# A delta rule and a feed-forward block on one core: the first pair's feed-forward in plain fp32, its weights split a pair later

## The chip, the core and the metric

The kernel runs on one core of a Trainium2 chip. The core has five engines that run side by side: TensorE (PE in the profile; its weight loads are PEld), VectorE (DVE), ScalarE (ACT), GpSimd (POOL) and SyncE (SP), which here only issues DMAs. Each engine goes through its own list of instructions in order and waits on semaphores. The metric is the device time of one execution in microseconds, the median of several; lower is better.

## The reference

Two steps. First a delta rule: for each of 32 sequences (4 batches of 8 heads) a 48 x 48 state is read and updated 768 times.

```python
for t in range(S):
    y[:, :, t] = np.einsum('bhd,bhde->bhe', q[:, :, t], state)
    v_old = np.einsum('bhde,bhd->bhe', state, kt)
    state = state + bt[:, :, :, None] * np.einsum('bhd,bhe->bhde', kt, vt - v_old)
```

Here `kt` is the key divided by its norm and `bt` is beta. The 3072 tokens of `y`, 384 wide, then go through a feed-forward block: `h = x @ w_in` (384 x 2048), `g` is 0 for h below -1, h for h above 1 and (h + 1)^2 / 4 between, and the result is `g @ w_out` (2048 x 384). The weights arrive as 64-bit floats, all else as fp32.

## The kernel before, in words

The sequences are cut into 12 chunks of 64 steps. Inside a chunk the recurrence is a triangular system, which is solved once for the chunk, and only the state goes from chunk to chunk. Two chunks make a pair (`G` = 0 to 5), which holds 512 tokens.

**The chain of a chunk** `g` is a row of small products on TensorE, each evicted by ScalarE or VectorE: `gram_k` and `gram_q` (products of keys with keys and with queries), `lanes` (norms, and the system laid out along the partitions), `solve` (the triangular inverse, on VectorE alone), `unlanes` (back again), merges that join inverted blocks, then `chain_r` (the state read with the keys), `chain_u`, `chain_y` (the chunk's output, which are the tokens of the feed-forward, evicted into the tile `xb` in two fp32r halves and completed by DMAs, line 434) and `chain_d` (the state's update). For pairs below `WHOLE` = 2 the inverse is made for blocks of 16 (15 steps, lines 284 and 286) and joined by `merge16_a` and `merge16_b` (lines 329, 341), then by `merge32_a` and `merge32_b` (line 358). From the third pair on it is made for blocks of 32 at once (30 steps, lines 295 and 297), and only the 32-merges follow.

**The feed-forward** of a pair is 16 items, one for each 128 of the 2048 columns. `up` (line 568) makes h, 128 x 512 in PSUM; ScalarE and VectorE make g from it (relu at 697 twice, square at 715, maximum with h at 723); `rest` (692, 693) cuts g into two fp32r halves; `down` (line 583) adds g times the second weights onto four accumulators, two items later (`LAG`). Both products are made in three fp32r passes: high by high, high by low, low by high (`PASSES`), so `up` is nine matmuls and `down` twelve. In the first pair six items are done in halves of 256 tokens (`LEAD`), since only the first chunk's tokens are there when it begins: 22 items.

**The weights** are turned from 64-bit floats into two fp32r halves by `weight` (lines 143 to 161), five operations for each of the 16 tiles: ScalarE scales the high word (149), GpSimd multiplies it to leave its sign (150), VectorE joins the words (152, 154), ScalarE copies the high half (158) and VectorE subtracts it (160). `unpack` deals these out, some in the prelude and two for each item after. Ten tiles are loaded at the start (`HOLD`), six later.

**The order of the work.** The engines' lists are written by hand (`manual_schedule`). The prelude does the whole chain of the first chunk and part of the second's. Each `stage` issues its products, then some steps of the weights, then its evictions. From then on the items are the clock: `plan` puts each chain step of the next pair at half an item's grid (`at`), TensorE's products into `pe` and the rest into `fill`, and the loop at the end issues them between an item's parts. An engine's step that waits holds all that stands behind it on that engine. `hold` (line 516) multiplies 18 times by zeros of 512 columns while the first inverse is made.

## Time and profile before

| what | us |
|---|---|
| three runs | 639.39, 639.80, 642.06 |
| their median | 639.8 |
| the profiled execution | 640.92 |
| its span (first to last instruction) | 639.2 |
| TensorE busy | 582.3 (91%) |
| VectorE busy | 451.9 (71%) |
| ScalarE busy | 387.6 (61%) |
| GpSimd busy | 101.6 (16%) |

How to read the rows that follow. A row of windows gives a stretch's start and end and its length, then for each engine its busy time and, after the x, how many instructions began in it; then the TensorE clock that was granted (1.00 is full), the share of the DMA engines' time, and GB/s. A row of the timeline gives start and duration, engine, line, operation, output<-input and shape, and in brackets the idle time before it with what ended that. A row of groups gives line, engine, operation, tiles, shapes and count, then the busy time in all and the mean of one in ns, then the engine's idle time before them. A plain fp32 matmul is two records on TensorE, an fp32r one is one.

### The profile page before, as it was taken

The numbers are of one execution on the slowest core, as the hardware profiler recorded it, in microseconds if no ns is written. First come the engines' busy times: TensorE is split into PE (matmuls) and PEld (weight loads), VectorE is DVE, ScalarE is ACT, GpSimd is POOL, SyncE is SP. The second block draws the span as 40 slices with busy tenths as digits, with TensorE's granted clock in tenths as the row PEclk, the third lists the DMA queues.
The fourth block names the chain that finished last, engine by engine and source line by source line (L and its number), as shares of the span: only waits on it lengthen the run. The fifth ranks groups of instructions, "written<-read, shape, count | busy, mean of one in ns | idle before, by whom it ended". The sixth has DMA issues, their size and how long they took to land.

```text
span 639.2 us, 21003 instructions
## 1 busy us (share of the span) xinstructions
PE 582.3 (91%) x9158; PEld 499.8 (78%) x9158; DVE 451.9 (71%) x921; ACT 387.6 (61%) x696; POOL 101.6 (16%) x119
## 2 busy tenths in 40 slices
PE   9944588897988999999999999999999999999996
PEld 7443477676877787888987888978888878899995
DVE  6999479795486598785897866997948973533332
ACT  4145567753664766656766657656667577566663
POOL 3458525300000400001200004000012000000000
PEclk9955689697999999999999999999999999999998
DMA  7914353000014210015210043200052000010002
GB/s 241 417 48 151 120 184 110 1 26 3 4 28 125 84 50 28 2 40 168 73 31 4 2 121 90 74 27 4 24 147 79 11 3 2 19 45 14 1 2 49
DMA packets 21100, 42.35 MB, mean 66 GB/s; under 512 B 4624, under 2 KB 10128, under 8 KB 21008
## 3 DMA queue, kind: packets, MB, share of 16 engines
q1 hardware_dynamic: 20144, 40.14, 20.4%
q8 instruction: 72, 1.18, 0.8%
q10 hardware_dynamic: 608, 0.79, 0.4%
q0 software_dynamic: 256, 0.08, 0.1%
q14 instruction: 20, 0.16, 0.1%
HBM read 33.91 MB, written 4.72 MB: 60 GB/s over the span
## 4 chain that ended last, share of the span: by engine, by line
PE 53%; DVE 32%; ACT 6%; issue 5%; DMA 1%; ACTq 0%; POOL 0%; SPq 0%; DVEq 0%
PE o L583 20%; PE h L568 18%; PE ch L175 8%; DVE glo L693 4%; DVE pr L295 3%; DVE A L297 3%; DVE s L723 3%; PE ch L420 3%; PE ch L358 2%; ACT ghi L692 2%; DVE wt L152 2%; ACT WQ L200 2%; DVE xb L154 2%; DVE pr L284 1%; DVE XT L305 1%
## 5 line engine op out<-in xcount | busy, mean ns | idle before, releaser
L568 PE MATMUL h<-xb,wt 128*128 128x512 f32 (+1 forms) x918 | 227.0, 392 | 9.3 <-DVE s L723 4.8
L583 PE MATMUL o<-wt,ghi 128*128 128x384 f32 x768 | 202.8, 346 | 0.8 <-ACT ghi L692 0.8
L568 PEld LDWEIGHTS h<-xb,wt 128*128 128x128 f32 x918 | 165.6, 192 | 42.4 <-DVE s L723 6.4
L583 PEld LDWEIGHTS o<-wt,ghi 128*128 128x128 f32 x768 | 138.1, 190 | 8.3 <-ACT ghi L692 1.5
L583 PE MATMUL o<-wt,glo 128*128 128x384 f32 x384 | 130.8, 341 | 0.0
L723 DVE TENSOR_TENSOR s<-h,s 128x512 f32<-128x512 f32 (+1 forms) x102 | 66.8, 655 | 89.6 <-ACT s L715 89.1
L692 ACT CAST ghi<-s 128x512 fp32r<-128x512 f32 (+1 forms) x102 | 60.8, 596 | 87.1 <-DVE s L723 77.6
L693 DVE TENSOR_TENSOR glo<-s,ghi 128x512 fp32r<-128x512 f32 (+1 forms) x102 | 68.7, 673 | 47.4 <-ACT ghi L692 46.0
L697 ACT ACTIVATE s<-h,half 128x512 f32<-128x512 f32 (+1 forms) x102 | 67.4, 661 | 50.7 <-PE h L568 50.0
L583 PEld LDWEIGHTS o<-wt,glo 128*128 128x128 f32 x384 | 73.0, 190 | 0.9 <-DVE glo L693 0.9
L697 ACT ACTIVATE s<-s,one 128x512 f32<-128x512 f32 (+1 forms) x102 | 71.4, 700 | 2.4
L715 ACT ACTIVATE s<-s 128x512 f32<-128x512 f32 (+1 forms) x102 | 61.9, 607 | 3.2
L208 POOL TENSOR_SCALAR_AFFINE_SELECT WQ<-WQ 64x512 f32<-64x512 f32 x48 | 34.2, 712 | 95.8 <-ACT WQ L200 93.3
L150 POOL TENSOR_SCALAR wt<-wt 128x768 f32<-128x768 f32 x16 | 39.2, 2454 | 41.6 <-ACT xb L149 41.2
L297 DVE TENSOR_TENSOR A<-A,pr 128x30 f32<-128x30 f32 (+14 forms) x120 | 40.9, 341 | 4.4
L295 DVE TENSOR_TENSOR pr<-A 128x30 f32<-128x30 f32 (+14 forms) x120 | 40.1, 334 | 1.4
L266 POOL TENSOR_SCALAR_AFFINE_SELECT A<-A 128x1024 f32<-128x1024 f32 x4 | 5.1, 1268 | 200.4 <-DVE A L265 200.4
L404 ACT COPY SU<-ch 64x384 f32<-64x384 f32 x46 | 21.8, 473 | 14.8 <-PE ch L175 14.1
L200 ACT COPY WQ<-ch 64x512 f32<-64x512 f32 x40 | 23.2, 580 | 7.4 <-PE ch L175 6.6
L420 PEld LDWEIGHTS ch<-WQ,SU 112*64 112x64 f32 x704 | 21.6, 138 | 4.6 <-ACT SU L404 3.4
L456 DVE TENSOR_TENSOR SU<-ch,SU 48x384 f32<-48x384 f32 x40 | 22.2, 555 | 3.4 <-PE ch L175 2.7
L420 PE MATMUL ch<-WQ,SU 112*64 112x64 f32 x704 | 23.1, 224 | 1.1 <-ACT SU L404 1.1
(130 smaller groups left out, 617.1 us busy)
## 6 DMA issues: line engine op xcount, KB each, us to landing
wt<-in_w_dram SPq DMA_DIRECT2D x16, 768.0 KB, 7.9
KV<-in_kv_dram SPq DMA_DIRECT2D x24, 384.0 KB, 4.5
out_dram<-wx SPq DMA_DIRECT2D x47, 96.0 KB, 2.2
WQ<-in_kqb_dram SPq DMA_DIRECT2D x24, 128.0 KB, 3.2
WK<-in_kqb_dram SPq DMA_DIRECT2D x24, 96.0 KB, 3.5
WQ<-in_kqa_dram SPq DMA_DIRECT2D x22, 96.0 KB, 2.8
xb<-X SPq DMA_DIRECT2D x63, 32.0 KB, 2.0
WK<-in_kqa_dram SPq DMA_DIRECT2D x20, 96.0 KB, 3.4
```

What stands on the lines that cost most here:

```text
L150: nc.gpsimd.tensor_scalar(out=st[:, :, 1::2], in0=st[:, :, 1::2], scalar1=0.0, scalar2=None, op0=ALU.mult)
L175: nc.tensor.matmul(tiles[i][dst:dst + l.shape[-1], v], l, r, start=True, stop=True)
L295: nc.vector.tensor_tensor(out=pr, in0=A[:, 0:n, j:j + 1].broadcast_to([P, n, m]), in1=A[:, j:j + 1, j + 1:32].broadcast_to([P, n, m]), op= ...
L297: nc.vector.tensor_tensor(out=A[:, 0:n, j + 1:32], in0=A[:, 0:n, j + 1:32], in1=pr, op=ALU.add)
L420: nc.tensor.matmul(yy[tk:tk + C, v // NP, v % NP], SF[rows, u:u + C], w_[rows, h, v, :], start=True, stop=True)
L568: nc.tensor.matmul(h[:, cols(bs)], WT[f][:, 0, x, k * P:(k + 1) * P], XB[G][:, y, k, cols(bs)], start=(n == 0), stop=(n == 8))
L583: nc.tensor.matmul(oacc[G, k], (ghi, glo)[x][:, k * P:(k + 1) * P], WT[f][:, 1, y, :], start=(new and n == 0), stop=(left[G, b] == 0 and n ...
L692: nc.scalar.copy(out=ghi[:, c], in_=s[:, c])
L693: nc.vector.tensor_tensor(out=glo[:, c], in0=s[:, c], in1=ghi[:, c], op=ALU.subtract)
L697: nc.scalar.activation(out=out, in_=in_, func=AF.Relu, bias=bias, scale=scale)
L715: nc.scalar.activation(out=s[:, c], in_=s[:, c], func=AF.Square)
L723: nc.vector.tensor_tensor(out=s[:, c], in0=h[:, c], in1=s[:, c], op=ALU.max)
```

## The change

- **The first pair's feed-forward is made in plain fp32.** `up` is three matmuls with the unsplit weights `W32` and the tokens `X32`, `down` four; the first two chunks' tokens are not split, and `rest` makes no halves for that pair. Four items are done in halves, twelve whole, four again in halves (`LEAD` = 4).
- **The weights are unpacked without GpSimd**: ScalarE makes both parts (`parts`: the low word's top three bits as an integer, and the scaled high word), VectorE joins them in two operations (`words`) into an fp32 tile that lies where an earlier tile's raw words were (`HOME`). The split into fp32r halves (`halves`) comes later, from item 13.5 of the first pair to item 9 of the second (`rework`). Pairs from the second on take the columns in the order `AGAIN`. All 16 tiles are loaded at the start, and the tables `ACT`, `PRE`, `GAIT` and `PACE` say how many steps of `parts` and `words` follow each stage and each half item.
- **Only the prelude inverts in blocks of 16** (`WHOLE` = 1); the second pair's chunks too are inverted whole, during the first pair.
- **Zeros** of 128 x 128 columns are multiplied: 80 while the first inverse is made, and 18 more spread over the prelude's stages (`HEAT`), two ahead of items (`HOT`).
- `chain_d` of the first chunk and `chain_r` of the second move from the first pair into the prelude, ahead of the first item.
- The ramp is two operations on ScalarE (relu of h/2 + 1/2, square) and one on VectorE (minimum with 1, maximum with h) in place of three and one.
- `plan` has tables for the first, the second and the later pairs in place of rules; the evictions of `merge32_b` are shared out otherwise, and the memsets in `merge32_a` are made in the prelude alone.

The core of the diff (of the tables one line stands):

```diff
-KEEP = 18
+KEEP = 80
-WHOLE = 2
-HOLD = 10
-LEAD = 6
+HOLD = 9
+LEAD = 4
+AHEAD = 8
+WHOLE = 1
...
-    weight_loads(2, HOLD)
+    weight_loads(2, FT)
...
-        nc.scalar.mul(out=x, in_=st[:, :, 1::2], mul=2.0 ** -112)
-        nc.gpsimd.tensor_scalar(out=st[:, :, 1::2], in0=st[:, :, 1::2], scalar1=0.0, scalar2=None, op0=ALU.mult)
-        yield
-        nc.vector.scalar_tensor_tensor(out=l, in0=l, scalar=29, in1=h, op0=ALU.logical_shift_right, op1=ALU.bitwise_or)
-        yield
-        nc.vector.scalar_tensor_tensor(out=xi, in0=xi, scalar=3, in1=l, op0=ALU.logical_shift_left, op1=ALU.bitwise_or)
...
+    def parts():
+        for f in range(FT):
+            by, wd, st = RAW[f].bitcast(U8), RAW[f].bitcast(I32), RAW[f]
+            nc.scalar.activation(out=wd[:, :, 0::2], in_=by[:, :, 3::8], func=AF.Identity, bias=floor, scale=2.0 ** -5)
+            yield
+            nc.scalar.mul(out=st[:, :, 1::2], in_=st[:, :, 1::2], mul=2.0 ** -112)
...
+    def words(f):
...
+        nc.vector.scalar_tensor_tensor(out=rest_, in0=top, scalar=-2 ** 31, in1=rest_, op0=ALU.bitwise_and, op1=ALU.bitwise_or)
+        yield
+        W32[f] = HOME[f]()
+        nc.vector.scalar_tensor_tensor(out=W32[f].bitcast(I32), in0=top, scalar=3, in1=rest_, op0=ALU.logical_shift_left, op1=ALU.bitwise_or)
+        yield
+    def halves(f, x):
+        both_ = const.tile([P, 2, 2, DM], F32R, name=f"wt{f}")
...
         nc.scalar.copy(out=hi, in_=x)
         yield
         nc.vector.tensor_tensor(out=lo, in0=x, in1=hi, op=ALU.subtract)
...
+        if g < 2:
+            def evict():
+                nc.scalar.copy(out=X32[:, :, c0:c0 + CT * C].rearrange("p k (b t) -> p b k t", t=C), in_=yy[:, :, 0:3])
...
     def stage(pieces, *fill):
         evicts = products(*pieces)
+        hold(next(E))
...
+    HEAT = [0, 1, 2, 5, 1, 2, 1, 0, 1, 2, 3, 0]
...
+    stage(one_(chain_d, 0), (pu, next(V)), (wu, next(W)))
+    load_kv(2)
+    stage(one_(chain_r, 1), (pu, next(V)), (wu, next(W)))
...
         for k in range(3):
+            if plain(G, f, bs):
+                nc.tensor.matmul(h[:, cols(bs)], W32[f][:, 0, k * P:(k + 1) * P], X32[:, k, cols(bs)], start=(k == 0), stop=(k == 2))
+                continue
...
+        passes = [((ghi, glo)[x], WT[f][:, 1, y]) for x, y in PASSES] if glo else [(ghi, W32[f][:, 1])]
...
+    STEADY = dict(ln=[-5.5, -4.5, -4.5, -4.5, -3.5, -2.5, -2.0], so=[-1.5, 5.5], un=[5.5, 6.0, 7.0, 9.5], va=[5.0, 5.5], vb=[11.0, 13.0], r=[6.5], m=[8.0, 9.0, 9.0, 10.5], kt=[2.5], K=[10.0, 11.0], T=[11.5, 12.0, 12.5, 13.0, 13.5, 14.0, 15.0], Q=[17.5, 17.0])
...
-        relu(s[:, c], h[:, c], half, -0.5)
+        relu(s[:, c], h[:, c], half, 0.5)
...
-        relu(s[:, c], s[:, c], one, -1.0)
         nc.scalar.activation(out=s[:, c], in_=s[:, c], func=AF.Square)
...
-        nc.vector.tensor_tensor(out=s[:, c], in0=h[:, c], in1=s[:, c], op=ALU.max)
+        nc.vector.scalar_tensor_tensor(out=s[:, c], in0=s[:, c], scalar=1.0, in1=h[:, c], op0=ALU.min, op1=ALU.max)
```

How the order changes, at three places. On VectorE in the prelude, from the copies of `merge32_a` to the first copies of `merge32_b` (XT is the inverse; wt and xb are weights), before:

```order
L371 COPY XT<-XT 32x16x32 x2
L152 SCALAR_TENSOR_TENSOR wt_112<-wt_112 128x768
L160 TENSOR_TENSOR wt_737<-xb,wt_737 128x2x384
L371 COPY XT<-XT 32x16x32 x2
L111 MEMSET wt_793 128x1
L154 SCALAR_TENSOR_TENSOR xb<-xb,wt_112 128x768
L152 SCALAR_TENSOR_TENSOR wt_114<-wt_114 128x768
L380 COPY XT<-o_800 32x8x32 x2
```

The same place of the changed kernel:

```order
L212 COPY XT<-XT 32x16x32 x4
L171 SCALAR_TENSOR_TENSOR wt_114<-wt_114 128x768
L421 COPY XT<-ch 32x8x32 x2
L266 TENSOR_TENSOR KV<-KV,N_289 128x384 x2
L174 SCALAR_TENSOR_TENSOR wt_112<-wt_114 128x2x384
L421 COPY XT<-ch 32x8x32 x2
```

Of the weights' operations ahead of the first of these copies, one is left of four.

On VectorE in the first pair, from one item's maximum to the next while the inverse for the second pair is made (pr and X are the inverse), before:

```order
L723 TENSOR_TENSOR s<-h,s 128x512
L160 TENSOR_TENSOR wt_1611<-xb,wt_1611 128x2x384
L284 TENSOR_TENSOR pr<-X,A_1614 128x78
L286 TENSOR_TENSOR X<-X,pr 128x2x3x13
L284 TENSOR_TENSOR pr<-X,A_1614 128x96
L286 TENSOR_TENSOR X<-X,pr 128x2x4x12
L693 TENSOR_TENSOR glo<-s,ghi 128x512
L154 SCALAR_TENSOR_TENSOR xb<-xb,wt_1105 128x768
L284 TENSOR_TENSOR pr<-X,A_1614 128x110
```

In the changed kernel (A is the inverse, made in blocks of 32; sixteen such rows stand between the first maximum and the next):

```order
L775 SCALAR_TENSOR_TENSOR s<-s,h 128x512
L324 TENSOR_TENSOR pr<-A 128x150
L326 TENSOR_TENSOR A<-A,pr 128x6x25
L324 TENSOR_TENSOR pr<-A 128x168
L326 TENSOR_TENSOR A<-A,pr 128x7x24
L324 TENSOR_TENSOR pr<-A 128x184
L326 TENSOR_TENSOR A<-A,pr 128x8x23
L324 TENSOR_TENSOR pr<-A 128x198
```

The weights' operations and the residual of g are gone from between the steps, and there are twice as many steps to an item.

On VectorE at the start of the second pair (lines 295 and 297, then 324 and 326, are the inverse for the third pair), before:

```order
L723 TENSOR_TENSOR s<-h,s 128x512
L295 TENSOR_TENSOR pr<-A 128x234
L297 TENSOR_TENSOR A<-A,pr 128x18x13
L693 TENSOR_TENSOR glo<-s,ghi 128x512
L295 TENSOR_TENSOR pr<-A 128x228
L297 TENSOR_TENSOR A<-A,pr 128x19x12
L295 TENSOR_TENSOR pr<-A 128x220
L297 TENSOR_TENSOR A<-A,pr 128x20x11
L230 TENSOR_TENSOR KV<-KV,N_2668 128x384
```

And the same steps in the changed kernel, where line 183 is the subtraction that splits a weight:

```order
L775 SCALAR_TENSOR_TENSOR s<-s,h 128x512
L324 TENSOR_TENSOR pr<-A 128x228
L326 TENSOR_TENSOR A<-A,pr 128x19x12
L324 TENSOR_TENSOR pr<-A 128x220
L326 TENSOR_TENSOR A<-A,pr 128x20x11
L739 TENSOR_TENSOR glo<-s,ghi 128x512
L183 TENSOR_TENSOR wt_2668<-wt_126,wt_2668 128x2x384
L324 TENSOR_TENSOR pr<-A 128x210
L326 TENSOR_TENSOR A<-A,pr 128x21x10
L324 TENSOR_TENSOR pr<-A 128x198
L326 TENSOR_TENSOR A<-A,pr 128x22x9
```

An item there has four steps where it had three, and a subtraction of a weight besides.

More of the change, by code (lines that the diff above doesn't have):

```diff
@@ L160, in weight, with unpack, rework @@
         nc.vector.tensor_tensor(out=lo, in0=x, in1=hi, op=ALU.subtract)
+        WT[f] = both_
         yield
+    def unpack():
+        for f in range(FT):
+            yield from words(f)
+    def rework():
+        for f in AGAIN:
+            yield from halves(f, W32.pop(f))
     pairs = ((0, C, C, 0), (C, 0, 0, 1))
@@ L553, in delta_rule_moe @@
         else:
-            items += [(G, f, (0, 1)) for f in range(FT)]
+            items += [(G, f, (0, 1)) for f in AGAIN]
     left = {}
@@ L565, in up @@
         n = 0
+        if G == 0 and HOT:
+            for _ in range(HOT.pop(0)):
+                nc.tensor.matmul(h[:, 0:P], warm, warm, start=True, stop=True)
         for k in range(3):
+            if plain(G, f, bs):
+                nc.tensor.matmul(h[:, cols(bs)], W32[f][:, 0, k * P:(k + 1) * P], X32[:, k, cols(bs)], start=(k == 0), stop=(k == 2))
+                continue
             for x, y in PASSES:
@@ L581, in down @@
                     new = False
-                for n, (x, y) in enumerate(PASSES):
-                    nc.tensor.matmul(oacc[G, k], (ghi, glo)[x][:, k * P:(k + 1) * P], WT[f][:, 1, y, :],
-                                     start=(new and n == 0), stop=(left[G, b] == 0 and n == 2))
+                for n, (x, y) in enumerate(passes):
+                    nc.tensor.matmul(oacc[G, k], x[:, k * P:(k + 1) * P], y, start=(new and n == 0),
+                                     stop=(left[G, b] == 0 and n == len(passes) - 1))
     def store(G, b):
@@ new lines, in plan @@
+        steps(scale_v(a), p["va"])
+        steps(scale_v(b), p["vb"])
+        if G == 0:
+            I = OPEN["I"]
+            at(pe, G, I[0], one(chain_u, 1))
+            at(pe, G, I[1], *both(chain_y, 1))
+            at(pe, G, I[2], one(chain_d, 1))
+            for t, f, g in zip(I[3:], (gram_k, gram_k, gram_q, gram_q), (a, b, a, b)):
+                at(pe, G, t, one(f, g))
+            at(fill, G, OPEN["L"][0], (load_q, 3))
+            at(fill, G, OPEN["L"][1], (load_kv, 3))
+            t, d = OPEN["W"]
+            steps(rework(), [t + int(j * d * 2) / 2 for j in range(2 * FT)])
@@ L688, in rest @@
     def rest(item, s):
+        if plain(*item):
+            gs[item] = s, None
+            return
         ghi = sb.tile([P, 2 * NB], F32R, name="ghi", bufs=2)
```

332 lines of the change are left out of this document (162 added, 170 removed).

## The prediction

> **What bounds the kernel now.** I read the profile from the outside in: first how busy each engine is in the six stretches between the first up-products of one pair and the next, then the stretch that is worst. The rows are the prelude, the first pair, the second, the third (the fourth is like it), the fifth, and the last with the tail.
>
> ```profile
> core 0: us, PE busy (x) PEld busy (x) DVE busy (x) ACT busy (x) POOL busy (x), PEclk, DMA share, GB/s
> 0.00:73.15 73.15, 48.55 (x1200) 35.21 (x1201) 62.78 (x110) 31.55 (x54) 42.17 (x38) 0.76 0.55 199
> 73.15:213.81 140.66, 119.84 (x2491) 102.51 (x2491) 98.42 (x203) 80.98 (x161) 28.23 (x32) 0.90 0.24 70
> 213.81:299.83 86.02, 84.48 (x1287) 73.16 (x1285) 67.84 (x148) 56.24 (x102) 7.47 (x13) 1.00 0.15 45
> 299.83:388.75 88.92, 87.72 (x1361) 76.09 (x1361) 70.12 (x152) 58.52 (x106) 8.84 (x15) 1.00 0.21 57
> ...
> 477.69:561.54 83.85, 82.62 (x1106) 72.30 (x1105) 56.93 (x118) 56.61 (x101) 6.07 (x10) 1.00 0.11 27
> 561.54:639.20 77.66, 71.29 (x361) 64.41 (x360) 25.68 (x38) 45.23 (x70) 0.00 (x0) 0.97 0.09 21
> ```
>
> From 213.81 us on, TensorE is idle for 1.2 to 1.5 us in each pair at a granted clock of 1.00: that part is its own, and only less work on TensorE could shorten it. The first two stretches are another matter. They hold 213.8 us, with 45 us of idle TensorE and clocks of 0.76 and 0.90. All that can be won lies there. The timeline shows what stands in the prelude's way.
>
> ```profile
> 49.58 1.41 PE L358 MATMUL o<-GG 32*32 32x32 f32 x60
> 54.66 1.55 DVE L371 COPY XT<-XT 32x512 f32<-32x512 f32 x2
> 56.37 1.17 DVE L154 SCALAR_TENSOR_TENSOR xb<-xb,wt 128x768 int32<-128x768 int32 x1
> 57.45 1.40 DVE L152 SCALAR_TENSOR_TENSOR wt<-wt 128x768 int32<-128x768 int32 x1
> 58.88 0.42 DVE L380 COPY XT<-o 32x256 f32<-32x256 f32 x1
> 65.06 2.36 PE L420 MATMUL h<-WQ,SU 64*64 64x64 f32 x31 [2.91 <-ACT SU L404]
> 73.15 0.98 PE L568 MATMUL h<-xb,wt 128*128 128x256 f32 x3 [4.21 <-DMA xb<-X]
> 75.92 1.53 PE L175 MATMUL ch<-SU,KV 64*48 64x48 f32 x64
> 81.36 2.29 PE L568 MATMUL h<-xb,wt 128*128 128x256 f32 x9
> ```
>
> The last merge stage's first product was done at 51.0 us, and VectorE copied it out only from 58.88, behind the weights' integer operations. Then the first up-product waited 4.21 us for a DMA, with the state's update and the next chunk's read queued behind it until 81.36.
>
> **The change, part by part.** Durations come from these groups and stretches (the first window holds line 518 alone, the second line 568 alone).
>
> ```profile
> 9.20 0.91 SPq L112 DMA_DIRECT2D wt<-in_w_dram  x2
> ...
> 18.00:30.00 12.00, 12.00 (x29) 5.30 (x28) 1.00 1.02 420
> 561.54:624.22 62.68, 33.81 (x135) 25.20 (x136) 1.00 0.06 14
> 16.00:32.00 16.00, 15.51 (x143) 7.13 (x144) 14.65 (x39) 2.98 (x4) 7.67 (x4) 1.00 1.02 418
> 32.00:73.15 41.15, 18.38 (x808) 16.13 (x797) 37.47 (x51) 21.61 (x38) 28.91 (x21) 0.57 0.30 98
> L693 DVE TENSOR_TENSOR glo<-s,ghi 128x512 fp32r<-128x512 f32 x90 | 61.9, 688 | 37.3 <-ACT ghi L692 36.2
> L723 DVE TENSOR_TENSOR s<-h,s 128x512 f32<-128x512 f32 x90 | 61.8, 687 | 72.6 <-ACT s L715 72.2
> L697 ACT ACTIVATE s<-s,one 128x512 f32<-128x512 f32 x90 | 65.3, 725 | 2.2
> L152 DVE SCALAR_TENSOR_TENSOR wt<-wt 128x768 int32<-128x768 int32 x16 | 17.0, 1064 | 0.0
> L160 DVE TENSOR_TENSOR wt<-xb,wt 128x768 fp32r<-128x768 f32 x16 | 16.5, 1032 | 0.0
> L149 ACT ACTIVATE xb<-wt 128x768 f32<-128x768 f32 x16 | 14.4, 907 | 12.3 <-DVE wt L160 7.0 <-DMA wt<-in_w_dram 4.5 <-ACT wt L158 0.8
> L297 DVE TENSOR_TENSOR A<-A,pr 128x30 f32<-128x30 f32 (+14 forms) x120 | 40.9, 341 | 4.4
> L295 DVE TENSOR_TENSOR pr<-A 128x30 f32<-128x30 f32 (+14 forms) x120 | 40.1, 334 | 1.4
> L265 DVE SCALAR_TENSOR_TENSOR A<-A,gm 128x1024 f32<-128x1024 f32 x4 | 4.9, 1219 | 0.0
> L303 DVE TENSOR_TENSOR A<-A,gm 128x1024 f32<-128x1024 f32 x4 | 4.9, 1218 | 0.0
> ```
>
> *Plain fp32 in the first pair.* The second row is line 518, the old zeros in plain fp32 with 512 columns: 28 weight loads in 12.00 us, 0.429 us for each record, and a plain matmul makes two records (36 for 18 matmuls). The third is line 568 in the last pair: 135 records are 15 items of nine, so an item in three fp32r passes takes 62.68/15 = 4.18 us. A plain item is three matmuls of 512 columns and four of 384: 6 x 0.429 + 8 x 0.322 = 5.15 us. Sixteen items are 82.4 us of TensorE where 66.9 stood: **15.5 us more**. [...]
>
> *The prelude.* GpSimd's multiply is gone, ScalarE makes both parts, and VectorE has two operations for a weight, not three. ScalarE needs 2 x 0.907 = 1.81 us for a weight. All sixteen are now requested at once, from 9.20 us on; 786 KB at 418 GB/s is 1.88 us, so with 1.6 MB of keys and values among them they land up to about 44 us, and ScalarE goes at the pace of the landings. The evictions of the first and of the third merge stage stand behind its operations on the tenth and the fifteenth weight, so at about 35 and 46 us. The fourth stage's first product can then follow at 48 and be done before the 51.0 of now: this costs nothing as long as the loads keep that rate. On VectorE only one weight operation stands before the copy that began at 58.88; of the 7.9 us from 51.0 the copies need 1.55, one operation about 1, so I take 5, and 3 more for the subtractions that are gone before. That makes 8, with the bounds 0 and 11. The state's update and the next read now stand ahead of the first item, over its DMA: the 4.21 us of waiting go, and the first item's 2.77 us (73.15 to 75.92) move behind. The first item then starts at 81.36 - 8 - 4.2 - 2.8 = **66 us**. The zeros between merges are 18 matmuls of 128 columns, 0.21 to 0.43 us each (a quarter of 0.86, or twice that at half clock), so 4 to 8 us in all, in gaps that the row from 32.00 shows to be wide (TensorE 18.38 busy of 41.15); I take no cost.
>
> *The first pair.* A full pair's chain work on TensorE is 88.92 - 66.9 = 22.0 us. Here it is 14 groups of products for 10 and three chunks' outputs for two; a group is about 1.15 us (the row at 98.20, below) and an output about 2.2 (2.36 for half of one at the prelude's half clock, above), so 22.0 + 4.6 + 2.2 = 28.8. With the items: 111.2 us. VectorE has the third pair's 70.1, less 16 x 0.688 for residuals that plain fp32 lacks, plus the second chunk's copies and additions and a second set of norms (an estimate, 13), eight word operations (8), eight split subtractions (8 x 1.032) and two fifths of the next solve (8): 96 us. Neither fits the other everywhere. Items 6 to 9.5 hold the whole solve of 32 columns: (40.9 + 40.1)/4 = 20.2 us, some 2 us of gaps and 3.5 x 0.687 make 24.7 on VectorE, against 3.5 x 5.15 + 1.15 = 19.2 on TensorE: 5.5 us idle. I add 3 for a half clock at the start and 3 for the second pair's tokens, whose chain ends 2.5 items before they are used. The pair: **123 us**, bounds 113 and 136. What hid the old merges of 16 goes with them: four groups of products and their evictions are not there any more.
>
> *The second pair* takes one more product group (1.15) and the rest of the splitting. In four items VectorE has 0.687 + 0.688 + 1.032 + about 2.6 of solve and 0.3 of gaps = 5.3 us against 4.18: about 4 us. ScalarE's casts have room (56.24 of 86.02). 86.0 + 1.2 + 4.1 = **91.3**, bounds 88 and 98. If the subtractions found idle time, the cost is nothing; the cover would be the old slack of 18 us.
>
> *The rest.* The new ramp drops a ScalarE operation of 0.725 us for each item; TensorE does not wait there, so only the end gains it: 77.0. The new maximum has three operands; lines 265 and 303 show the same 1.22 us for both forms, so nothing. The steady tables are re-timed: 1.2 us of idle in each pair can be won, and a solve squeezed into seven items can lose as much: 177.9 for the third and fourth, 85.0 for the fifth, which takes one product group. Bounds: 4 either way.
>
> Sum of the span: 66 + 123 + 91.3 + 177.9 + 85.0 + 77.0 = 620.2 us. The profiled execution took 640.92 with a span of 639.2, so 1.7 lie around it: 621.9. It lay 1.1 above the median of 639.8, so the forecast is **621 us**.
>
> **The rivals.** Their rows:
>
> ```profile
> 73.15:81.15 8.00, 6.19 (x137) 5.38 (x137) 0.83 (x2) 4.06 (x9) 1.77 (x4) 0.50 0.62 173
> 113.15:121.15 8.00, 5.30 (x13) 3.33 (x12) 5.45 (x15) 6.01 (x12) 2.62 (x4) 0.50 0.00 0
> 98.20 1.16 PE L175 MATMUL ch<-WK 48*64 48x64 f32 x64
> 122.82:142.54 19.72, 4.46 (x15) 0.99 0.04 12
> 122.82:142.54 19.72, 3.83 (x15) 0.99 0.04 12
> 147.34 1.90 PE L329 MATMUL ch<-XT,GG 32*32 32x16 f32 x128 [3.67 <-DVE KV L390]
> 164.54 0.85 PE L358 MATMUL ch<-XT,GG 32*32 32x32 f32 x64
> ```
>
> *Full clock (0.22).* The zeros keep the array at 1.00 through the prelude. TensorE's 18.38 us at 0.57 would be 10.5; of those 7.9 I put 5 on the path: 61. A first pair that runs warm with its solve covered takes 113, the second 88. 61 + 113 + 88 + 177.9 + 85 + 77 = 601.9, so 603 us. For it: dense zeros held 1.00 from 18 to 30 us. Against it: 18 short matmuls over 25 us are thin. [...]
>
> *The chain sets the pair: slower (0.12).* The place is VectorE's queue in the first pair. There the half solve (the two rows of 19.72 us, lines 284 and 286) is 8.3 us of work and took 19.7, 2.4 times as long, with items and weights between its steps. If the whole solve stretches alike, 20.2 becomes 48.5: 29 more, less the 17.2 of the old merges (147.34 to 164.54), plus 8.3 of subtractions. It began 23.5 us after the second key product ended (99.36), which is 18 after the reads did (81.36); from 66 that makes 84 now, and 107.5 for the solve. From there to the second pair it was 213.81 - 122.82 = 91; now 91 + 29 - 17.2 + 8.3 = 111, so 218.5 and a pair of 152, 29 more than the forecast's: 650 us. It is slower from a first pair of 145 us on, a solve of more than 40 us. For it: VectorE is busy 37.47 of 41.15 in the prelude. Against it: the order puts seven or eight steps of the solve between two maxima, where two stood.
>
> *Zeros or ScalarE on the path (0.10).* The change does not do what it says in the prelude: the filling's 8 us, or a late weight ahead of an eviction, eat the gain, and the first item starts at 73: 628 us.
>
> **How the numbers follow.** Forecast 0.56, full clock 0.22, late prelude 0.10, slow chain 0.12. A measurement here tells 0.5%, 3.2 us, from no change. The forecast's own bounds (113 to 136 for the pair, 4 either way elsewhere) reach 607 to 638. The range 602 to 638 takes in most of the full clock's case too; what it leaves out is the rest of that (0.08) and the slow chain (0.11). Faster: 0.54 + 0.22 + 0.08 = 0.84; same 0.05; slower 0.11.
>
> **What would show it.** The first up-product stands near 66 us, and a plain item's fourteen records at 0.43 and 0.32. The first pair is near 123 us, with TensorE idle during the solve; VectorE is over 95% busy there and at the start of the second pair. The third and fourth pairs stay within 2 us of 88.9. It is wrong if the second pair starts after 200 us or before 180, if the first item comes after 70, or if the later pairs move by more than 2 us each.

## The result, and the profile after

The changed kernel takes 611.1 us (the median of 609.6, 611.1 and 613.1), the kernel before 640.7 in the same session: a ratio of 0.954, with a 95% interval of 0.950 to 0.959. The forecast was 621, with a range of 602 to 638. A fourth execution of the changed kernel ran at a granted clock of 0.565 and took 912 us; it is left out of these figures, and the profile below is of a later execution (611.9 us, span 610.2).

The windows of the changed kernel, cut where those of before were cut: the prelude, the pairs one to five, and the last pair with the tail.

```profile
core 0: us, PE busy (x) PEld busy (x) DVE busy (x) ACT busy (x) POOL busy (x), PEclk, DMA share, GB/s
0.00:72.52 72.52, 58.32 (x1489) 53.43 (x1489) 51.40 (x97) 45.69 (x71) 17.66 (x30) 0.76 0.62 230
72.52:184.08 111.56, 110.19 (x1590) 68.17 (x1589) 90.70 (x195) 49.40 (x98) 8.28 (x12) 0.98 0.21 57
184.08:273.16 89.08, 87.34 (x1347) 73.53 (x1345) 77.29 (x150) 52.94 (x96) 7.00 (x10) 1.00 0.19 54
273.16:360.85 87.69, 87.69 (x1362) 76.19 (x1362) 71.25 (x153) 46.95 (x89) 6.83 (x10) 1.00 0.21 58
...
448.49:532.56 84.07, 84.07 (x1170) 73.59 (x1169) 59.87 (x126) 45.87 (x86) 5.40 (x8) 1.00 0.11 31
532.56:610.22 77.66, 71.31 (x361) 64.48 (x360) 25.06 (x38) 33.42 (x53) 0.00 (x0) 0.99 0.09 21
```

| stretch | before | forecast | after |
|---|---|---|---|
| until the first up-product | 73.15 | 66 | 72.52 |
| first pair | 140.66 | 123 | 111.56 |
| second pair | 86.02 | 91.3 | 89.08 |
| third and fourth | 177.86 | 177.9 | 175.33 |
| fifth | 83.85 | 85.0 | 84.07 |
| last, and the tail | 77.66 | 77.0 | 77.66 |
| span | 639.20 | 620.2 | 610.22 |

By these windows the first pair gives all of it: 29.1 of 29.0 us. TensorE is idle there for 1.4 us, where it was for 20.8, and its clock is 0.98, not 0.90. The prelude gives 0.6 us, not 7. But the first item does not stand at the same work in both kernels, since `chain_d` and `chain_r` moved ahead of it. Counted from the end of that `chain_r` (81.36 us before, 72.52 now), 8.8 us are won ahead of it and 20.9 in the rest of the first pair. The sum came out 10 us too high by misses of both signs: 6.5 too low for the prelude, 11.4 too high for the first pair, and 5.1 too high for all that follows. So part of the closeness of 621 is luck.

The prelude on TensorE, by the timeline: the zeros (551) and the merges of 16 (372, 382).

```profile
start us, us, engine line op out<-in xcount [idle before <-releaser]
12.41 19.44 PE L551 MATMUL o<-wx 128*128 128x128 f32 x160
31.77 1.23 PE L372 MATMUL ch<-XT,GG 32*32 32x16 f32 x126
...
32.87 0.60 PE L372 MATMUL h<-XT,GG 32*32 32x16 f32 x48
38.31 1.26 PE L372 MATMUL h<-XT,GG 32*32 32x16 f32 x78 [4.84 <-issue]
39.51 0.80 PE L551 MATMUL o<-wx 128*128 128x128 f32 x2
40.23 0.84 PE L382 MATMUL h<-xb,XT 32*32 32x16 f32 x48
44.66 1.26 PE L382 MATMUL h<-xb,XT 32*32 32x16 f32 x80 [3.60 <-issue]
...
48.67 1.36 PE L382 MATMUL o<-xb,XT 32*32 32x16 f32 x84 [0.83 <-issue]
```

Three stops stand here, 9.3 us in all, and none waits for another engine: "issue" is time in which TensorE waited for nothing that the profile shows. They come at a fixed distance: from the stop of 4.84 to that of 3.60 there are 78 + 2 + 48 = 128 records. A record goes with one weight load (1489 of each in the first window above), so that is 256 instructions by the profile's counts. The DMA view of 30 to 60 us has a queue for instructions:

```profile
DMA  9999999999999999999984200010000100000000
...
q8 instruction: 6, 0.10, 1.6%
```

Queue q8 moved six packets, 0.10 MB in all, so about 16 KB each; and until 45 us the DMA engines are full with weights (the 9s). No view names what a stop waits for. This gave the two theories of the prelude: a late block of instructions, or, as the forecast had it, the queues of VectorE and ScalarE.

Such stops stood in the kernel before as well, in its merges of 16 (329, 341):

```profile
35.87 1.30 PE L329 MATMUL h<-XT,GG 32*32 32x16 f32 x81 [3.12 <-issue]
39.47 1.30 PE L341 MATMUL h<-A,XT 32*32 32x16 f32 x82 [1.70 <-issue]
...
42.92 1.36 PE L341 MATMUL o<-A,XT 32*32 32x16 f32 x83 [1.55 <-issue]
```

There they come to 6.4 us, so they grew by 2.9. In the view of 34 to 44 us of that kernel q8 moved two packets, in the slices from 36.75 and from 40.50 us, 0.9 and 1.0 us behind the ends of two stops: one packet to 128 records. What differs more is the distance from one stop's end to the next: 3.60 and 3.45 us before, where the DMA engines were nearly idle (a share of 0.02 from 36 to 44 us), and 6.35 us in the changed kernel, where weights were still landing, then 4.01. The merges of 16 end at 44.28 us before and at 50.03 now.

### The profile page after: what moved, and what is told of

Its sections match the earlier page's. It is cut to its first block, busy times and chain, and to the rows that moved or that the text cites. A ratio compares the mean times of both kernels' runs of the same rounds, so it can differ in the third digit from the quotient of the medians.

```text
span 910.3 us, 19840 instructions
## 1 busy us (share of the span) xinstructions
PE 899.4 (99%) x8668; PEld 607.3 (67%) x8668; DVE 444.7 (49%) x907; ACT 325.5 (36%) x582; POOL 51.6 (6%) x80
## 4 chain that ended last, share of the span: by engine, by line
PE 97%; DMA 1%; issue 0%; ACTq 0%; ACT 0%; SPq 0%; DVE 0%
PE o L632 38%; PE h L616 30%; PE ch L208 9%; PE h L613 8%; PE o L551 4%; PE ch L461 4%; PE ch L399 2%; PE o L461 0%; DMA WK<-in_kqa_dram 0%; PE h L208 0%; DMA WQ<-in_kqa_dram 0%; ACTq L469 0%; PE o L382 0%; PE h L382 0%; PE o L399 0%
## 5 line engine op out<-in xcount | busy, mean ns | idle before, releaser
L616 PE MATMUL h<-xb,wt 128*128 128x512 f32 x720 | 285.5, 564 | 0.0
L632 PE MATMUL o<-wt,ghi 128*128 128x384 f32 x672 | 257.7, 477 | 0.0
L632 PE MATMUL o<-wt,glo 128*128 128x384 f32 x360 | 176.6, 510 | 0.0
L775 DVE SCALAR_TENSOR_TENSOR s<-s,h 128x512 f32<-128x512 f32 (+1 forms) x87 | 58.8, 676 | 119.7 <-ACT s L767 119.2
L739 DVE TENSOR_TENSOR glo<-s,ghi 128x512 fp32r<-128x512 f32 x80 | 57.1, 714 | 77.6 <-ACT ghi L738 75.9
L738 ACT CAST ghi<-s 128x512 fp32r<-128x512 f32 x80 | 49.5, 619 | 102.2 <-PE o L632 93.6
L613 PE MATMUL h<-xb,wt 128*128 128x512 f32 (+1 forms) x102 | 67.7, 829 | 0.0
L326 DVE TENSOR_TENSOR A<-A,pr 128x30 f32<-128x30 f32 (+9 forms) x150 | 50.1, 334 | 5.5
L324 DVE TENSOR_TENSOR pr<-A 128x30 f32<-128x30 f32 (+9 forms) x150 | 49.3, 329 | 4.3 <-POOL A L313 1.4
L551 PE MATMUL o<-wx 128*128 128x128 f32 x196 | 41.8, 400 | 0.0
L445 ACT COPY SU<-ch 64x384 f32<-64x384 f32 x44 | 20.8, 473 | 44.6 <-PE ch L208 43.9
```

Of the source, the lines that this page charges most:

```text
L326: nc.vector.tensor_tensor(out=A[:, 0:n, j + 1:32], in0=A[:, 0:n, j + 1:32], in1=pr, op=ALU.add)
L551: nc.tensor.matmul(idle, warm, warm, start=True, stop=True)
L613: nc.tensor.matmul(h[:, cols(bs)], W32[f][:, 0, k * P:(k + 1) * P], X32[:, k, cols(bs)], start=(k == 0), stop=(k == 2))
L616: nc.tensor.matmul(h[:, cols(bs)], WT[f][:, 0, x, k * P:(k + 1) * P], XB[G][:, y, k, cols(bs)], start=(n == 0), stop=(n == 8))
L632: nc.tensor.matmul(oacc[G, k], x[:, k * P:(k + 1) * P], y, start=(new and n == 0), stop=(left[G, b] == 0 and n == len(passes) - 1))
L738: nc.scalar.copy(out=ghi[:, c], in_=s[:, c])
```

## The experiments

All ratios are to the kernel before in the same session (641.5 to 642.2 us at the median); the numbers in brackets are 95% intervals. "More" and "less" are against the changed kernel, which was run once more, beside three of the experiments: 611.8 us, 0.953 (0.950 to 0.957).

> The changed kernel as it stands, for a trace in which the clock is undisturbed. The forecast expects the first up-product near 66 us, a first pair of 123 us with TensorE idle during the solve, and a second pair of 91.3; the full-clock case expects 61, 113 and 88 with a granted clock near 1.00 in the prelude. Either way about 611 us in all, so where the forecast's 621 was too long must show in these three stretches.

The first three stretches hold 7.1 of the 10 us by which the sum was too long; the other 2.8 lie behind them.

**No zeros in the gaps.**

```diff
-    HEAT = [0, 1, 2, 5, 1, 2, 1, 0, 1, 2, 3, 0]
+    HEAT = [0] * 12
-    HOT = [0, 0, 0, 0, 0, 0, 1, 1]
+    HOT = []
```

> The 18 zero products between the prelude's stages and the two ahead of items are left out; the 80 during the first inverse stay. The forecast gave them no cost and no gain: within 2 us of the changed kernel, so 609 to 613. The full-clock case says that they hold the clock: without them the prelude's clock falls to about 0.57 and the time rises by 5 us or more, to 616 or above. Zeros on the path: faster by 2 to 8 us.

Measured 611.1 us, 0.9525 (0.950 to 0.955), the same as with them. From 32 us to the first item, with the zeros and then without:

```profile
32.00:72.52 40.52, 29.37 (x1057) 25.89 (x1045) 27.33 (x37) 26.57 (x45) 5.67 (x8) 0.62 0.41 159
```
```profile
32.00:71.93 39.93, 23.79 (x1031) 21.11 (x1029) 27.80 (x38) 27.02 (x46) 5.65 (x8) 0.56 0.43 165
```

Fewer zeros and a lower clock (0.56 for 0.62) leave the stretch as long: neither the cost of these zeros nor the clock that they hold decides anything. What the zeros took, the stops take without them: they are 4.78, 4.18, 1.55, 1.53 and 0.70 us there, 12.7 in all and not 9.3. In the trace of the changed kernel the granted clock is 0.96 from 32 to 36 us and 0.50 from 36 us on, in the stop of 4.84 that ends at 38.31. It is still there long after: from 52 to 66 us TensorE is busy almost without a break by the profile (13.99 of 14.00 us), at 0.50. Why is not shown.

**Less TensorE work in the first pair.** Only two of a plain up-product's three matmuls are made, 13.7 us less; the output lacks a third of `x @ w_in` for that pair.

```diff
-                nc.tensor.matmul(h[:, cols(bs)], W32[f][:, 0, k * P:(k + 1) * P], X32[:, k, cols(bs)], start=(k == 0), stop=(k == 2))
+                if k < 2:
+                    nc.tensor.matmul(h[:, cols(bs)], W32[f][:, 0, k * P:(k + 1) * P], X32[:, k, cols(bs)], start=(k == 0), stop=(k == 1))
```

> One of the three matmuls of each up-product in the first pair is left out (a third of x @ w_in is missing for those tokens), so TensorE has 16 x 0.857 = 13.7 us less there and no other engine has less. If TensorE sets the first pair throughout (full clock), the time falls by 13 to 14 us, to 597 or 598. By the forecast TensorE waits during the 3.5 items of the solve and at the end, so some 9 to 10 us, to 602. If the chain on VectorE sets the pair, less than 3 us.

Measured 606.5 us, 0.945 (0.942 to 0.948): 5.3 us less. The first pair:

```profile
72.82:178.20 105.38, 97.13 (x1549) 60.24 (x1549) 89.62 (x194) 49.49 (x98) 8.46 (x12) 0.99 0.21 60
```

The pair falls by 6.2 us of the 13.7, and TensorE is then idle for 8.2. That is none of the three expected amounts (13 to 14, 9 to 10, less than 3). In the changed kernel TensorE is the bound in the first pair, and some 6 us below it another bound follows. TensorE's waits here are nearly all for VectorE: 4.5 us for its maxima (line 776) and 2.2 for the additions to the state (line 508).

**One item of lag.** In the first pair an item's output products follow its maximum by one item, not by two.

```diff
-        if len(ready) == LAG:
+        if len(ready) == (1 if item[0] == 0 else LAG):
```

> In the first pair the output products of an item follow its maximum by one item, not by two; the other pairs keep two. Question: why the solve of 24.8 us on VectorE did not stop TensorE (idle 0.38 us at its end), where 5.5 us were forecast. Theory 1 (TensorE lives through it on the lag: VectorE starts the solve up to two items ahead and ends it as late as it may): with one item less of lead, 5.15 us are gone from a reserve that was used up but for 0.4, so TensorE stops for about 4 to 5 us in items 6 to 10 and perhaps 1 to 3 at other places; the first pair takes 116 to 119 us instead of 111.6, the rest as before, in all 4 to 8 us slower. Rival (TensorE's own product groups between the items cover the solve, and the lag plays no part): the first pair stays within 1.5 us of 111.6, and the time within 2 us.

Measured 615.1 us, 0.958 (0.955 to 0.961), 3.2 to 3.5 us more. The pair and its stops during and after the solve:

```profile
71.79:186.97 115.18, 111.57 (x1594) 68.64 (x1592) 90.41 (x195) 49.34 (x98) 8.26 (x12) 0.99 0.19 56
```
```profile
121.63 2.85 PE L632 MATMUL o<-wt,glo 128*128 128x384 f32 x8 [0.95 <-DVE glo L775]
128.75 2.85 PE L632 MATMUL o<-wt,s 128*128 128x384 f32 x8 [0.61 <-DVE s L775]
135.22 2.85 PE L632 MATMUL o<-wt,ghi 128*128 128x384 f32 x8 [1.06 <-DVE ghi L775]
```

With the lag cut, output products wait for VectorE's maxima in the solve's items, where only one up-product had waited, for 0.38 us. The pair rose by 3.6 us, a little under what the theory gave (4.4 to 7.4); the rival's "within 1.5" is out. The lag was a cover, but not all of the 5.5 us hung on it.

**The old ramp** (three operations on ScalarE, a maximum of two tensors on VectorE).

```diff
-    relu(s[:, c], h[:, c], half, 0.5)
+    relu(s[:, c], h[:, c], half, -0.5)
...
+    relu(s[:, c], s[:, c], one, -1.0)
     nc.scalar.activation(out=s[:, c], in_=s[:, c], func=AF.Square)
...
-    nc.vector.scalar_tensor_tensor(out=s[:, c], in0=s[:, c], scalar=1.0, in1=h[:, c], op0=ALU.min, op1=ALU.max)
+    nc.vector.tensor_tensor(out=s[:, c], in0=h[:, c], in1=s[:, c], op=ALU.max)
```

> The ramp is made as before, in three operations on ScalarE and a two-operand maximum; all else as changed. The forecast: TensorE does not wait for the ramp, so only the end loses the 0.7 us, 611.5 to 612.5. The rival: the shorter ramp frees h sooner where VectorE is behind, in the first two pairs; then 3 us or more are lost, 614 or above.

Measured 617.4 us, 0.962 (0.959 to 0.966): 5.5 us more. The second, the third and the last stretch:

```profile
183.37:274.19 90.82, 88.20 (x1345) 73.92 (x1346) 77.39 (x150) 64.53 (x112) 7.02 (x10) 1.00 0.19 53
274.19:362.61 88.42, 88.36 (x1361) 76.60 (x1361) 71.63 (x153) 58.44 (x105) 7.04 (x10) 1.00 0.20 57
...
535.43:613.70 78.27, 71.77 (x361) 64.78 (x360) 25.66 (x38) 45.20 (x70) 0.00 (x0) 0.99 0.09 21
```

It costs 1.7 us in the second pair and 0.3 to 0.8 in every other, not only at the end. ScalarE is far from full (58 of 88 us), but its third operation, 0.72 us, stands ahead of each item's maximum. How that delay becomes time is only seen in part. TensorE's waits for the maxima in the second pair are 1.2 us, against 1.0 in the changed kernel. In the third it waits for almost nothing (0.06 us idle), and its busy time is longer (88.36 for 87.69).

**The split's subtraction on GpSimd.**

```diff
-        nc.vector.tensor_tensor(out=lo, in0=x, in1=hi, op=ALU.subtract)
+        nc.gpsimd.tensor_tensor(out=lo, in0=x, in1=hi, op=ALU.subtract)
```

> The split's subtraction (sixteen of them, in the second pair) is made by GpSimd and no longer by VectorE. Prices from the run of the changed kernel: its second pair takes 89.08 us, the third 87.69, so 1.4 us are lost in the second. Theory 1 (VectorE's queue is what loses them): VectorE is rid of 16 x 1.03 = 16.5 us of its 77.3, the second pair comes to 87.7 us, and the kernel gains 1.4 us. Rival (the loss lies in the start of the pair, before its first item's products, or in GpSimd working beside VectorE): the second pair stays at 89 us or rises; if GpSimd stretches VectorE's work or is late with a weight, to 91 or more.

Measured 616.1 us, 0.960 (0.957 to 0.963): 4.3 us more, and the second pair takes 94.15 us, not 89.08. Theory 1 falls, the rival holds. The groups on VectorE at the pair's start, changed kernel first, then this one, and GpSimd's:

```profile
L326 DVE TENSOR_TENSOR A<-A,pr 128x198 f32<-128x198 f32 (+14 forms) x22 | 9.1, 412 | 0.8
L324 DVE TENSOR_TENSOR pr<-A 128x210 f32<-128x210 f32 (+14 forms) x21 | 8.7, 415 | 0.4
```
```profile
L326 DVE TENSOR_TENSOR A<-A,pr 128x198 f32<-128x198 f32 (+14 forms) x22 | 14.6, 664 | 0.8
L324 DVE TENSOR_TENSOR pr<-A 128x198 f32<-128x198 f32 (+14 forms) x22 | 11.1, 507 | 0.4
```
```profile
L183 POOL TENSOR_TENSOR wt<-wt,wt 128x768 fp32r<-128x768 f32 x8 | 15.8, 1974 | 18.6 <-ACT wt L181 18.6
```

VectorE is rid of 0.95 us for a weight, but its solve's operations take 664 and 507 ns where they took 412 and 415, with GpSimd's subtractions beside them. The GpSimd multiply of the kernel before shows something alike: beside one that runs from 35.50 to 37.74 us, VectorE's operation on a weight at 35.55 took 1.64 us, and 0.94 at 31.70 us with none beside it. No run puts the multiply back alone.

**The old timings in the steady table.**

```diff
-    STEADY = dict(ln=[-5.5, -4.5, -4.5, -4.5, -3.5, -2.5, -2.0], so=[-1.5, 5.5], un=[5.5, 6.0, 7.0, 9.5],
+    STEADY = dict(ln=[-5.5, -5.0, -5.0, -4.5, -4.5, -4.0, -4.0], so=[-3.5, 7.0], un=[7.0, 7.5, 8.0, 8.5],
...
```

> Only the numbers of the steady table are put back to those of the kernel before (norms from -5.5 to -4, the solve from -3.5 to 7, and so on); all else is the changed kernel. Theory 1 (the new numbers are what took 1.3 us from each later pair, 88.9 to 87.65): third and fourth pair 88.9 us again, the fifth about as now, in all 2.5 us slower than the changed kernel, up to 4. Rival (the shorter ScalarE ramp is what took it; the run with the old ramp showed 88.4 and 88.4): with the old numbers the pairs stay within 0.4 us of 87.7, and the time within 1 us.

Measured 625.2 us, 0.974 (0.971 to 0.977): 13.4 us more, far beyond theory 1's own bound of 4. The second to the fourth pair, and TensorE's longest wait in the second:

```profile
182.69:280.10 97.41, 90.38 (x1408) 76.36 (x1409) 78.56 (x156) 54.56 (x99) 8.34 (x13) 0.98 0.18 51
280.10:371.55 91.45, 89.48 (x1361) 77.09 (x1361) 69.77 (x152) 47.69 (x90) 6.64 (x11) 0.98 0.20 55
371.55:461.69 90.14, 88.17 (x1361) 76.33 (x1361) 69.79 (x152) 47.72 (x90) 6.67 (x11) 1.00 0.20 56
```
```profile
PE ch L399 <- DVE XT L334: 3.0, 1, 3.0
```

The old numbers begin the inverse's way back (`un`) at 7, close ahead of the merges of 32 at 8; the new ones begin it at 5.5. In the second pair, where VectorE also splits weights, TensorE then waits 3.0 us for the transposed inverse (line 334). That wait costs more than its length: the granted clock is 0.92 on average from 222 to 244 us, and 1.00 in the stretches on both sides. One product group (64 records, about 1.15 us) also lies in the second pair here (1408 records for 1347) and in the fifth of the changed kernel, so that much of the 8.3 us is only moved. The third and fourth pairs are longer than in the kernel before with the same numbers (88.9); so the new table is needed with the other edits, and its worth is not the 1.3 us that a pair fell.

**Six loads out.** The loads of the last six weight tiles are left out and GpSimd writes zeros in their place; the output lacks those weights.

```diff
-            nc.sync.dma_start(out=RAW[f].bitcast(I32), in_=w.bitcast(I32)[:, f])
+            if f < 10:
+                nc.sync.dma_start(out=RAW[f].bitcast(I32), in_=w.bitcast(I32)[:, f])
...
     run(ln)
+    for f in range(10, FT):
+        nc.gpsimd.memset(RAW[f], 0.0)
```

> The loads of the last six of the sixteen weight tiles are left out; GpSimd writes zeros into their tiles instead, and all that is computed on them stays in the program (the output lacks those weights). Question: what held the merges of 16 and 32 in the changed kernel's prelude, where TensorE stood for 4.84, 3.60 and 0.83 us with nothing in the profile to wait for, after every 128 records. Theory 1 (the next block of TensorE's instructions comes late, because it lands behind the weights in the same DMA engines): with the DMA engines empty from about 33 us on, these stops shrink to the 0.7 to 1.7 us that they were in the kernel before where no weights were landing; the first item comes at 68 us (66.5 to 70) instead of 72.5, the time falls by 3 to 5 us. Rival (ScalarE's and VectorE's queues pace the merges, and TensorE's stops only fall into their wait): the stops shrink too, but the first item stays within 1 us of 72.5.

Measured 606.3 us, 0.945 (0.942 to 0.948): 5.5 us less. The same places of the timeline as above:

```profile
37.03 1.13 PE L373 MATMUL h<-XT,GG 32*32 32x16 f32 x78 [2.17 <-issue]
...
40.90 1.26 PE L383 MATMUL h<-xb,XT 32*32 32x16 f32 x80 [1.25 <-issue]
...
44.63 1.36 PE L383 MATMUL o<-xb,XT 32*32 32x16 f32 x84 [0.56 <-issue]
...
68.21 2.93 PE L616 MATMUL h<-xb 128*128 128x256 f32 x6
```

The stops are at the same records and come to 4.0 us, not 9.3, and their ends stand 3.87 and 3.73 us apart; the first item follows at 68.2, not 72.5. That is 4.3 us for 5.3 us of stops: theory 1.

**Six loads late.** The same loads wait for a small VectorE memset behind the merges of 16; ScalarE's operations on them move behind the merges of 32.

```diff
+            if f >= LATE:
+                nc.vector.memset(RAW[f][:, 0, 0:1], 0.0)
...
     stage(one_(merge16_b, 1), (pu, next(V)), (wu, next(W)))
+    weight_loads(LATE, FT)
...
-    ACT = [0, 1, 0, 5, 1, 4, 0, 1, 5, 0, 1, 2, 4]
+    ACT = [0, 1, 0, 1, 0, 0, 0, 0, 2, 2, 2, 2, 2]
```

> A version meant to be used: the loads of the last six weight tiles are held back until after the four merges of 16 (each waits for a small VectorE memset, as in the kernel before), and ScalarE's operations on them move behind the merges of 32, into the chain's stages and the first items. Theory 1 (the late instruction blocks set the merges): the stops of 4.84 and 3.60 us shrink to 0.7 to 1.7, the merges of 16 end 5 us sooner; the late loads then meet the merges of 32 and the chain, and may give 1 to 3 us back there. First item at 69 us (67 to 72), the time 2 to 4 us below the changed kernel's. Rival (the merges are paced by VectorE's and ScalarE's queues): first item at 72 to 75 us, since the last weights come later and nothing else is won; same time or slower by up to 2 us.

Measured 615.9 us, 0.960 (0.957 to 0.964): 4 us more. The stops moved with the loads:

```profile
39.94 1.26 PE L385 MATMUL h<-xb,XT 32*32 32x16 f32 x80 [0.80 <-issue]
...
54.42 0.75 PE L402 MATMUL ch<-GG 32*32 32x32 f32 x36 [2.77 <-issue]
...
60.96 1.32 PE L211 MATMUL h<-KV,XT 64*64 64x48 f32 x40 [3.12 <-issue]
...
72.64 0.31 PE L211 MATMUL ch<-SU,WK 48*64 48x48 f32 x2 [2.84 <-ACT SU L506]
```

Where 3.60 stood, 0.80 is left; the merges of 32 and `chain_u` (the state's update in the words of two expectations below), which had none, stop for 2.77 and 3.12 us with the six loads now requested just ahead of them. The stops go with the loads. That the instructions themselves land late behind the weights fits this and the packets of q8, but remains the author's reading. As a version to be used it failed: the first item came at 75.6 us, later than either theory gave (67 to 72, and 72 to 75). The new stops take back what the old ones gave, and ScalarE's moved operations also hold up the state's copies (2.84 us, where the changed kernel waits 1.31).

**Six loads behind the prelude,** so that they land during the first items; ScalarE's and VectorE's steps on them move into items 2.5 to 13.5.

```diff
     load_k(3)
+    weight_loads(LATE, FT)
...
-    GAIT = [4, 2, 1, 2, 3, 0, 1, 1, 2, 0, 3, 0, 3, 1]
+    GAIT = [0] * 5 + [1] * 12
```

> A second attempt at a version meant to be used. The run in which the held loads came right behind the merges of 16 only moved TensorE's stops (4.84, 3.60 and 0.83 us became 2.45, 0.80 and 0.29, and two new ones of 2.77 and 3.12 us appeared in the merges of 32 and the state's update, while the six loads were landing). Here the six loads are requested behind everything else of the prelude, so that they land during the first items; ScalarE's two operations on them go to items 2.5 to 8, VectorE's to items 3.5 to 5.5 and 10 to 13.5. Theory 1 (a block of 256 instructions, 128 records of plain fp32, comes late when weights are landing): the prelude goes as in the run with six loads left out, first item at 68 to 69 us; in the first pair TensorE issues 128 records in 25 us or more outside the product groups, so the loads cost there 0 to 2 us; the first pair takes 112 to 114, since VectorE gets six more weight operations (5.7 us) where it has some 5 us to spare; in all 607 to 609 us, 3 to 5 below the changed kernel. Rival (the merges are not what sets the first item, or the loads, the state's rows and the next keys collide at 66 to 80 us): first item at 71 us or later, or the first pair at 116 or more; no gain.

Measured 617.2 us, 0.961 (0.957 to 0.965): 5.4 us more. The first item came at 67.96 us, as theory 1 had it, but the first pair took 123.6. SyncE's issue of the second chunk's rows in the changed kernel, then here, and who waits:

```profile
80.93 3.73 SPq L469 DMA_DIRECT2D xb<-stg  x6
```
```profile
76.83 8.38 SPq L472 DMA_DIRECT2D xb<-stg  x6
```
```profile
89.58 4.57 PE L617 MATMUL h<-xb 128*128 128x512 f32 x6 [5.93 <-DMA xb<-stg]
```

Behind six loads the rows took 8.4 us to issue where they took 3.7, and TensorE stood 5.9 us for them, then ran its next up-product at a granted clock of 0.50 (4.57 us for 2.84). TensorE also waits 1.5 us there for a weight that VectorE joins late and 1.8 for a maximum. So the rival's collision was right for the pair.

**A shorter hold.** 67 zeros, not 80, while the first inverse is made.

```diff
-KEEP = 80
+KEEP = 67
```

> The zeros that TensorE multiplies while it waits for the solve of 16 are 67 matmuls, not 80 (0.243 us each, so 3.2 us less). In the changed kernel they ran until 31.85 us, while VectorE had written the merges' operand by 29.53: 2.3 us of zeros stood on the path, which no term of the forecast has. Theory 1 (they cost what they last): the merges begin at 29.6, each later step follows, first item at 70.2, time 2.3 us below the changed kernel's. Rival (the next block of TensorE's instructions sets the merges, and it lands with the weights whenever TensorE asks for it): the merges begin at 29.6, but the stop of 4.84 us grows to about 7, and the first item stays within 0.7 us of 72.5; no gain.

Measured 610.3 us, 0.951 (0.950 to 0.953). VectorE's last write of the merges' operand in the changed kernel (done at 29.53, while the zeros quoted above ran until 31.85), then the hold and the stops here:

```profile
28.46 1.07 DVE L360 STREAM_TRANSPOSE XT<-A 128x512 f32<-128x512 f32 x1
```
```profile
11.95 16.40 PE L551 MATMUL o<-wx 128*128 128x128 f32 x134
34.86 0.93 PE L372 MATMUL h<-XT,GG 32*32 32x16 f32 x52 [4.60 <-issue]
...
41.20 0.94 PE L382 MATMUL h<-xb,XT 32*32 32x16 f32 x54 [2.11 <-issue]
...
47.40 1.03 PE L382 MATMUL o<-xb,XT 32*32 32x16 f32 x58 [3.02 <-issue]
```

The stops are no shorter (9.7 us for these three; their ends stand 6.34 and 6.20 us apart, while weights land), but all comes earlier, and the first item stands at 70.55: theory 1 by the profile. In the other runs that leave the prelude as it is, it stood between 71.1 and 72.8, so the gain lies little outside their scatter, and the two ratios (0.951 and 0.953) cannot be told apart.

**Both: 67 zeros, and the six loads one at a time,** behind stages from the second merge of 16 to `chain_u`.

```diff
+    weight_loads(LATE + 0, LATE + 1)
     stage(one_(merge16_b, 0), (pu, next(V)), (wu, next(W)))
+    weight_loads(LATE + 1, LATE + 2)
...
-    GAIT = [4, 2, 1, 2, 3, 0, 1, 1, 2, 0, 3, 0, 3, 1]
+    GAIT = [2, 1, 1, 1, 1]
```

> The last attempt at a version meant to be used: 67 zeros as in the run beside it, and the last six weights requested one at a time, behind the second, third and fourth merge of 16, the second and fourth merge of 32 and the state's update (VectorE's memset releases each), with ScalarE's operations on them moved to where they have landed. Requested all at once behind the merges of 16, they stopped TensorE for 2.77 and 3.12 us; left out, the stops of the merges of 16 shrank from 9.3 us to 4.0; requested behind the whole prelude, they held up the second chunk's rows on SyncE's queue for 5.9 us. Theory 1 (what delays a block of instructions is how much is queued ahead of it in the DMA engines, so one load of 1.9 us costs at most 1 to 2 us where six cost 3): the stops come to 6 to 7 us in all instead of 9.3, merges from 29.6 us on, first item at 67 to 69, first pair 112 as now, time 607 to 609. Rival (the loads fill the gaps anyway and every block waits for one of them): first item at 71 or later, time no lower than the run beside it.

Measured 610.3 us, 0.951 (0.949 to 0.953). A wait for ScalarE and a stop that the spaced loads left:

```profile
65.06 0.31 PE L211 MATMUL ch<-SU,WK 48*64 48x48 f32 x2 [2.03 <-ACT SU L506]
...
75.11 2.21 PE L464 MATMUL ch<-WQ,SU 112*64 112x64 f32 x64 [1.78 <-issue]
```

The first item stands at 68.3, as theory 1 gave, and the first pair takes 113.4: the stop of 1.78 us now falls into the second chunk's output. The time is that of the shorter hold alone, as the rival had it, and not 607 to 609. No version here beats the changed kernel by more than a measurement tells.

## Why the forecast was right in sign, and where it failed

- **The prelude: 66 forecast, 72.5 measured.** The term that failed is the 8 us for VectorE's queue. The read that ended at 81.36 before now ends at 72.5, 8.8 us earlier; by the sum's own terms 4.2 and 2.8 of these are the wait and the first item's part, so of the 8 only 1.8 came. VectorE's queue was shorter, as said: before, VectorE copied the last merge stage's first product 7.9 us after it was done, and now 1.3 us after it (57.36 to 58.62). But the forecast had that product "done before the 51.0 of now", and it was done at 57.36, because TensorE had become the late one: with all 16 loads requested at once it stops for 9.3 us after blocks of 128 records (4.0 with six loads out, and 4.3 us of the first item given back). I had costed the loads on ScalarE alone and let "this costs nothing as long as the loads keep that rate" stand, without asking what else they move (the instructions of q8, 1.6% of their time from 30 to 60 us); yet rows with "issue" stood in the trace of before, too. Another part is the hold: no term had 80 zeros lasting 2.3 us longer than the solve.
- **The first pair: 123 forecast, 111.6 measured.** The TensorE floor of 111.2 (82.4 for plain items, 28.8 for the chain) was right to 1 us: TensorE is busy 110.2 us. What failed are the three additions. The 5.5 us for the solve: it did take 24.8 us on VectorE, from 102.65 to 127.5 against my 24.7, but I had let TensorE wait item by item, while the lag lets it run two items ahead; the stop was 0.4 us. With a lag of one the pair is 3.6 longer. The 3 for a half clock were about 1.5: the first up-product takes 2.29 us where later ones take 1.56, and the product behind it 1.96 for 1.15, at a granted clock of 0.65 from 72 to 76 us. The 3 for the second pair's tokens did not come: TensorE was idle for 1.4 us in all.
- **The clock.** Full clock was a rival with 0.22. The pair ran near full clock as it said (0.98; 111.6 us for 113), but the zeros between merges are not why: without them the first pair takes 110.8. Its prelude did not come: 72.5 us at a mean clock of 0.62 from 32 us on, where it had 61 at 1.00.
- **The second pair: 91.3 forecast, 89.1 measured.** It takes 1.4 us more than the third pair, where the sum had 4.1 for the split (its own rows give 4.5: four items of 5.3 against 4.18). No run leaves the split out, so its price alone is not shown.
- **The later pairs: nothing forecast, 1.3 us each gained.** The sign was left open and the bounds held; the old ramp gives 0.7 to 0.8 of it back. That the tables are neutral was wrong: with the old numbers the same edits lose 13 us.
- **The ramp: 0.7 us forecast, 5.5 measured.** The step that failed is "TensorE does not wait there, so only the end gains it". With the old ramp every stretch from the first pair on is longer, and the third pair by 0.7 us with TensorE hardly idle: the forecast took a busy TensorE for one that cannot be made faster. At the end, where the 0.7 was to come, the stretch is as long as before (77.66).
- **No cost for the zeros in gaps:** right. **The rivals:** the slow chain (VectorE stretched in the solve) did not appear: the solve took 24.8 us, about what the forecast had for its unstretched steps. The late prelude (first item at 73) did, for a reason of its own, and cost as much as that rival had.
- My own marks of failure: a first item after 70 came true, a second pair outside 180 to 200 did not (184.1), nor did later pairs that move by more than 2 us.

What stays open: which of the edits frees the first pair, since no run puts plain fp32, the unsplit weights or the whole solve back alone; where the longer ramp enters TensorE's busy time; why the old table loses 2.5 to 3.8 us in the third and fourth pairs, where its waits in the third come to 2.0 us and the only lower clock seen is 0.92 from 350.00 to 371.55 us; and which of VectorE's works, the maxima or the additions to the state, sets the pair some 6 us below TensorE's floor.

## What to carry to other kernels

Before all loads are moved to the start, look at which engine then runs many short instructions: here TensorE stopped after blocks of 128 records, for up to 4.84 us with weights landing and 1.70 us or less at a DMA share of 0.02, and "issue" stops at a fixed number of records are the sign. Zeros between the products only filled such stops here (9.3 us of stops with them, 12.7 without), and a shorter hold left them as long (9.7). Fewer loads beside the short instructions shortened them (4.0), but the loads then had to go somewhere else. When VectorE has a burst longer than TensorE's work beside it, count the items by which TensorE may run ahead before charging the difference. A step on a half-empty engine was not free where each item's result passes through it (ScalarE's 0.72 us for an item, with the other maximum, was 5.5 us of the time): ask what its latency costs, even where the consumer shows no idle time.
